# Sums of key-value features times query features: one 128-column product, or two 64-column products on the two halves of the array

## The chip, the cores and the metric

The kernel runs on one core of a Trainium2 chip. The metric is the device time of one execution in microseconds. The time before is 671.87 us, the median of three runs (671.34 to 672.88). One more execution was taken with the hardware profiler. It took 672.59 us, and every view of the profile below describes that execution.

## What is computed

A sequence of 2048 tokens with 512 features goes through a linear attention with 32 heads, and then through a mixture of eight experts of which each token uses one. All numbers are float32. The part that matters here, cut from the reference:

```python
phi_q = concatenate([softmax(pq), softmax(-pq)])      # 32 features per head and token
phi_k = concatenate([softmax(pk), softmax(-pk)])
kv  = einsum("bhsf,bhsd->bhfd", phi_k, v)             # 32 x 16 per head, summed over tokens
z   = einsum("bhsf->bhf", phi_k)
num = einsum("bhqf,bhfd->bhqd", phi_q, kv)
den = einsum("bhqf,bhf->bhq", phi_q, z)[..., None] + 1e-6
o   = num / den                                       # then o @ wo, a residual, and the experts
```

The change is in how `num` and `den` are made.

## The kernel before

The work is in stages, on 16 chunks of 128 tokens. In the first stage each chunk is projected to queries, keys and values, the feature maps are taken, and the sums `kv` and `z` grow in PSUM (the products of line 640). The query features are transposed, so that the features lie along the partitions and the tokens along the columns, and kept in SBUF as `phT[c]`: eight groups of 128 features (four heads of 32 features each) by 128 tokens (line 650).

When the sums are complete, they are copied to `kvbd` (line 814): for each of the eight groups a block-diagonal matrix of 128 features by 68 columns, four heads with 16 values and one denominator each.

Then comes the stage of the change, one step for each chunk `c` (the loop of line 940). It is a pipeline by hand: step `c` issues `s_num(c)`, `s_ot(c-1)` and `s_wo(c-2)`.

- `s_num(c)` (line 472) makes numerators and denominators. For two halves `i` of the heads it takes a PSUM bank `pn`, and TensorE makes four products into it (line 478). In each, the 128 features by 128 tokens of `phT` stand in the array, and the 68 columns of `kvbd` move through it. The result has 128 tokens as partitions and 68 columns. VectorE then takes the reciprocal of the denominators (`den`, line 482) and multiplies (`o`, line 483).
- `s_ot(c)` (line 487) transposes `o` on TensorE (`pto`, line 442). ScalarE rounds the result to its high part `xh` (line 78) and VectorE takes the rest `xl` (line 81).
- `s_wo(c)` (line 826) multiplies with the output weights in three products of high and low parts for each piece (`po`, lines 84 to 86, 24 instructions for a chunk). VectorE adds the residual (`hb`, line 838), and ScalarE and GpSimd make the statistics of the second norm.

Between them lie the small products of the token ranking (`pl`, lines 886 and 887; `acc`, line 908). From step 10 on, the weights of the first expert are loaded (`raw`, lines 253 and 981) and split into high and low parts by ScalarE, VectorE and GpSimd (lines 78 and 210). The experts follow and take the rest of the time; of them only the transposes of line 1132 play a part in the prediction, four of which have 32 tokens in place of 128.

Each engine takes its instructions in order. TensorE's loading of a standing operand (LDWEIGHTS, "PEld" in the profile) has rows of its own beside those of the products ("PE"). A product of plain float32 operands, such as `pn`, shows as two load rows and two product rows, so the 128 products of line 478 are 256 rows of each. A product of the rounded parts, such as `po`, shows as one of each. In the views, a form such as `128*32` ahead of the shape is the part of the array that an instruction uses, rows by columns.

Of the kernel before, what the change touches and what calls it, by code (L numbers as in the profile page):

```python
# [49 lines left out]
def kernel(  # L50
# [14 lines left out]
    V, A, G, T = nc.vector, nc.scalar, nc.gpsimd, nc.tensor  # L65
# [65 lines left out]
    def bank(name):  # L131
        return ps.tile([P, 512], F32, name=name, tag="b")
# [244 lines left out]
    with ExitStack() as actx:  # L377
# [23 lines left out]
        phT = [None] * NT  # L401
        for i in (3, 2, 1, 0):
# [3 lines left out]
            if i == 3:  # L406
                wohi = pool.tile([P, KD, 2, HC], F32R, name="wohi")
                wolo = pool.tile([P, KD, 2, HC], F32R, name="wolo")
                kvbd = pool.tile([P, NG, VC], F32, name="kvbd")
# [8 lines left out]
        st = [dict() for _ in range(NT)]  # L418

        def row(name, bufs, tag):  # L420
            return work.tile([P, D], F32, name=name, tag=tag, bufs=bufs)

        def load_x(c, queue=nc.sync):
            st[c]["xt"] = row("xt", 3, "xt")
            queue.dma_start(st[c]["xt"], x[c * P:(c + 1) * P, :])
# [46 lines left out]
        def s_num(c):  # L472
            load_x(c)
            o = row("o", 2, "pc").rearrange("p (h f) -> p h f", f=DH)
            for i in range(2):
                pn = bank("pn")
                for g in range(4):
                    st[c]["pn"] = T.matmul(pn[:, g * 68:(g + 1) * 68], phT[c][:, 4 * i + g, :],
                                           kvbd[:, 4 * i + g, :], start=True, stop=True)
                nv = pn[:, 0:272].rearrange("p (h f) -> p h f", f=DH + 1)  # L480
                den = work.tile([P, 16, 1], F32, name="den")
                V.reciprocal(den, nv[:, :, DH:DH + 1])
                V.tensor_tensor(o[:, 16 * i:16 * i + 16, :], nv[:, :, 0:DH],
                                den.to_broadcast([P, 16, DH]), op=OP.mult)
            st[c]["o"] = o.rearrange("p h f -> p (h f)")
# [5 lines left out]
        if True:  # L491
# [319 lines left out]
            with after(pin["f1"]):  # L811
                for i in range(2):
                    for h in range(4):
                        pin["kv"] = V.tensor_tensor(kvbd[32 * h:32 * h + 32, 4 * i:4 * i + 4, 17 * h:17 * h + 17],
                                                    kvps[i][32 * h:32 * h + 32, :, 17 * h:17 * h + 17],
                                                    epsz[32 * h:32 * h + 32], op=OP.add)
            s_num(0)
            s_num(1)
            s_ot(0)
            with after(pin["kv"]):  # L820
# [119 lines left out]
        for c in range(NT + 8):  # L940
            if c > 1:
                at(s_num, c)
                at(s_ot, c - 1)
# [447 lines left out]
```

## Time and profile before

| what | value |
|---|---|
| time, median of three runs | 671.87 us (671.34 to 672.88) |
| time of the profiled execution | 672.59 us |
| its span, first to last instruction | 670.9 us |
| TensorE granted clock, mean over the span | 0.994 |
| products of line 478 | first starts at 194.3 us, last at 270.3 us |
| ScalarE busy, share of the span | 54% |
| GpSimd busy, share of the span | 33% |

The profiled execution took 1.69 us more than its span, which lies before the first and after the last instruction. A row of a timeline names the start, the length, the engine, the line of the code, the operation, the tiles written and read, the shape and how many instructions were merged into it. A row's length includes the time that the result takes to arrive, so the rows of successive products overlap. The pace, which is the time from one start to the next, says what a product costs when they follow each other.

### The profile page before, as it was taken

How to read it: one execution, taken by the hardware profiler on the slowest of the kernel's cores; microseconds unless marked ns; L12 is line 12 of the kernel's file. 1: busy time of each engine (PE TensorE's matmuls, PEld its weight loads, DVE VectorE, ACT ScalarE, POOL GpSimd, SP SyncE). 2: the span in 40 equal slices, each digit the busy share in tenths (PEclk: the TensorE clock that was granted, in tenths of full speed). 3: DMA queues.
4: the chain of work that ended last, by engine and by line, in shares of the span. 5: the costliest groups of instructions: out<-in, count | busy, mean ns of one | idle time of the engine just before them, and what ended most of it. 6: DMA issues, size and time to landing. Idle time of an engine off the chain costs nothing. (4 is left out here: it accounts for less than half of the span.)

```text
span 670.9 us, 12045 instructions
## 1 busy us (share of the span) xinstructions
PE 657.4 (98%) x4151; PEld 584.9 (87%) x4151; DVE 474.9 (71%) x903; ACT 361.0 (54%) x589; POOL 221.4 (33%) x294
## 2 busy tenths in 40 slices
PE   9999999999999999999999999999999999999994
PEld 8899999999999999867888888888888999999883
DVE  7997898877877677885132799995495657675961
ACT  6554445544324436745112688884485556675750
POOL 4576566666525345741100111121102111310210
PEclk9999999999999999999999999999999999999997
DMA  9522120100001429717600589996286636664620
GB/s 327 178 80 80 64 79 17 33 16 1 1 1 32 128 88 354 282 64 254 248 3 32 196 346 349 351 387 256 62 339 246 221 128 227 224 229 145 224 88 21
DMA packets 25804, 107.33 MB, mean 160 GB/s; under 512 B 3358, under 2 KB 3358, under 8 KB 16768
## 3 DMA queue, kind: packets, MB, share of 16 engines
q1 hardware_dynamic: 22096, 95.49, 39.5%
q0 software_dynamic: 3488, 10.92, 4.7%
q8 instruction: 35, 0.57, 0.3%
q14 instruction: 41, 0.34, 0.2%
q10 hardware_dynamic: 144, 0.02, 0.0%
HBM read 98.00 MB, written 8.81 MB: 159 GB/s over the span
## 5 line engine op out<-in xcount | busy, mean ns | idle before, releaser
L210 DVE TENSOR_TENSOR wlo<-raw,whi 128x1024 fp32r<-128x1024 f32 (+1 forms) x143 | 165.9, 1188 | 27.6 <-ACT whi L78 25.2
L78 ACT ACTIVATE whi<-raw 128x1024 fp32r<-128x1024 f32 (+1 forms) x148 | 145.3, 1007 | 32.7 <-PE mh L86 23.1
L161 POOL DMA_INDIRECT out_dram<-xg,sidx x15 | 18.1, 1206 | 186.6 <-DVE xg L1137 103.5
L601 POOL TENSOR_TENSOR ph<-t,sm 128x1024 f32<-128x1024 f32 x32 | 62.0, 1938 | 37.7 <-DVE sm L599 37.4
L589 ACT ACTIVATE t<-t,rstd 128x1024 f32<-128x1024 f32 x32 | 36.7, 1145 | 42.7 <-DVE t L588 42.7
L195 ACT ACTIVATE hs<-mh 128x512 f32<-128x512 f32 (+1 forms) x52 | 28.0, 538 | 50.7 <-PE mh L86 49.9
L84 PE MATMUL my<-whi,hA 128*128 128x512 f32 x120 | 50.1, 417 | 0.0
L149 POOL DMA_INDIRECT xg<-hbuf,gidx x22 | 27.0, 1226 | 64.6 <-DMA out_dram<-xg,sidx 46.4
L86 PE MATMUL my<-whi,hA 128*128 128x512 f32 x120 | 47.3, 394 | 0.0
L85 PE MATMUL my<-wlo,hA 128*128 128x512 f32 x120 | 47.1, 393 | 0.0
L594 DVE TENSOR_REDUCE sm<-t 128x64 f32<-128x1024 f32 x32 | 38.9, 1215 | 8.0 <-ACT t L589 5.2
L81 DVE TENSOR_TENSOR hA<-mtr,hA 128x512 fp32r<-128x512 f32 (+1 forms) x38 | 22.7, 597 | 30.5 <-ACTq L1061 15.8
L84 PE MATMUL mh<-whi,xhi 128*128 128x512 f32 (+1 forms) x112 | 42.6, 381 | 0.0
L86 PE MATMUL mh<-whi,xlo 128*128 128x512 f32 (+1 forms) x112 | 41.2, 368 | 0.0
L85 PE MATMUL mh<-wlo,xhi 128*128 128x512 f32 (+1 forms) x112 | 41.2, 367 | 0.0
L84 PE MATMUL po<-wohi,xh 128*128 128x260 f32 x128 | 37.4, 293 | 0.7 <-ACT xh L78 0.6
L84 PE MATMUL pv<-wvhi,xh 128*128 128x260 f32 x128 | 36.4, 284 | 0.0
L85 PE MATMUL po<-wolo,xh 128*128 128x260 f32 x128 | 36.3, 284 | 0.0
L86 PE MATMUL po<-wohi,xl 128*128 128x260 f32 x128 | 36.3, 285 | 0.0
L85 PE MATMUL pv<-wvlo,xh 128*128 128x260 f32 x128 | 36.3, 283 | 0.0
L86 PE MATMUL pv<-wvhi,xl 128*128 128x260 f32 x128 | 36.2, 283 | 0.0
L84 PE MATMUL mh<-whi,xwh 128*128 128x512 f32 (+1 forms) x96 | 36.1, 376 | 0.0
(353 smaller groups left out, 1936.7 us busy)
## 6 DMA issues: line engine op xcount, KB each, us to landing
raw<-in_w_dram SPq DMA_DIRECT2D x70, 1024.0 KB, 5.5
xt<-in_x_dram SPq DMA_DIRECT2D x32, 256.0 KB, 2.8
hbuf<-hb SPq DMA_DIRECT2D x8, 515.0 KB, 3.5
xT<-in_xTs_dram SPq DMA_DIRECT2D x16, 256.0 KB, 2.7
phT<-in_wv_dram SPq DMA_DIRECT2D x4, 256.0 KB, 4.1
phT<-in_wqkT_dram SPq DMA_DIRECT2D x4, 256.0 KB, 5.1
phT<-in_wqkT_dram SPq DMA_DIRECT2D x2, 512.0 KB, 6.4
phT<-in_wo_dram SPq DMA_DIRECT2D x2, 512.0 KB, 8.1
```

Of the source, the lines that this page charges most:

```text
L78: return A.activation(dst, src, AF.Copy)
L81: return V.tensor_tensor(dst, src, hi.bitcast(F32), op=OP.subtract)
L84: T.matmul(ps, ahi, bhi, start=first, stop=False)
L85: T.matmul(ps, ahi, blo, start=False, stop=False)
L86: return T.matmul(ps, alo, bhi, start=False, stop=last)
L149: G.indirect_dma_start(out=dst[0:n, :], out_offset=None, in_=hbuf if col else hbuf[0:S // 2, :], in_offset=bass.IndirectOffsetOnAxis(ap=gi ...
L161: m = G.indirect_dma_start(out=out, out_offset=bass.IndirectOffsetOnAxis(ap=sidx[0:n, col:col + 1], axis=0), in_=src[0:n, 0:D], in_offset= ...
L195: return A.activation(hs[c % 2][:, 0:fw], p[:, 0:fw], AF.Silu)
L210: return eng.tensor_tensor(lo, r, h.bitcast(F32), op=OP.subtract)
L589: A.activation(t, t, AF.Exp, scale=st[c]["rstd"])
L594: m = V.tensor_reduce(sm, t, AX.X, OP.add)
L601: pin["f2"] = G.tensor_tensor(ph.rearrange("p (a f) -> p a f", f=DH), t, bc(sm, DH), op=OP.mult)
```

## The change

In `s_num` each product of 128 standing tokens becomes two of 64. The first has the tokens 0 to 63 standing and writes the partitions 0 to 63 of `pn`. The second has the tokens 64 to 127 and writes the partitions 64 to 127. The moving operand, 68 columns of `kvbd`, is the same for both. The results are the same numbers at the same places. Nothing else is touched.

```diff
             for i in range(2):
                 pn = bank("pn")
                 for g in range(4):
-                    st[c]["pn"] = T.matmul(pn[:, g * 68:(g + 1) * 68], phT[c][:, 4 * i + g, :],
-                                           kvbd[:, 4 * i + g, :], start=True, stop=True)
+                    for s in range(2):
+                        r = slice(64 * s, 64 * s + 64)
+                        st[c]["pn"] = T.matmul(pn[r, g * 68:(g + 1) * 68], phT[c][:, 4 * i + g, r],
+                                               kvbd[:, 4 * i + g, :], start=True, stop=True)
```

## The prediction

> **What bounds the kernel now.** I read the page first, then the stretch of the changed stage by windows, then TensorE's waits there, then single blocks of the timeline. The page's first rows:
>
> ```profile
> PE 657.4 (98%) x4151; PEld 584.9 (87%) x4151; DVE 474.9 (71%) x903; ACT 361.0 (54%) x589; POOL 221.4 (33%) x294
> ```
>
> TensorE is busy 98% of the span. That is an average, so the stage itself has to be asked. The windows below are successive steps of the chunk loop, each from the start of one chunk's `pn` products to the next. Columns: window, its length, busy time and rows of each engine, granted clock, DMA share, GB/s.
>
> ```profile
> core 0: us, PE busy (x) PEld busy (x) DVE busy (x) ACT busy (x) POOL busy (x), PEclk, DMA share, GB/s
> 221.02:226.29 5.27, 5.27 (x51) 5.22 (x49) 4.24 (x20) 2.02 (x5) 1.42 (x6) 1.00 0.21 50
> 226.29:231.53 5.24, 5.24 (x51) 5.20 (x49) 2.89 (x11) 2.02 (x5) 3.12 (x9) 1.00 0.39 119
> ...
> 263.29:268.58 5.29, 5.29 (x52) 5.23 (x50) 4.75 (x17) 5.29 (x13) 3.64 (x9) 1.00 1.01 349
> 268.58:273.81 5.23, 5.23 (x52) 5.19 (x49) 5.09 (x20) 3.51 (x9) 3.71 (x9) 1.00 1.00 416
> ```
>
> A step takes 5.2 to 5.3 us, PE is busy in all of it at full clock, and the next engine, DVE, in 55 to 97%. TensorE's waits from 180 to 300 us are one wait of 0.6 us and one of 0.3:
>
> ```profile
> PE po L84 <- ACT xh L78: 0.6, 1, 0.6
> PE selp L300 <- DVE raw L294: 0.3, 1, 0.3
> ```
>
> So in this stage TensorE sets the end, and time taken from or given to it there moves everything behind it. Next, what sets the pace of the changed products. One block (eight products, 16 rows), its loads, and what stands around it:
>
> ```profile
> 214.95 1.90 PE L478 MATMUL pn<-kvbd,phT 128*128 128x68 f32 x16
> 216.68 0.60 PE L442 MATMUL pto<-ident,o 128*128 128x128 f32 x4
> ```
>
> ```profile
> 214.83 1.87 PEld L478 LDWEIGHTS pn<-kvbd,phT 128*128 128x128 f32 x16
> ```
>
> Next pn's own rows in the view of the tile, with least, median and greatest length in ns, and a long run of plain float32 products:
>
> ```profile
> L478 PEld LDWEIGHTS pn<-kvbd,phT x256: 187/192/193, 194.1 to 270.2; 128*128 128x128 f32 x128
> L478 PE MATMUL pn<-kvbd,phT x256: 222/275/307, 194.3 to 270.3; 128*128 128x68 f32 x128
> ```
>
> ```profile
> 297.82 5.31 PE L1199 MATMUL my<-raw,raw 128*128 128x512 f32 x12
> ```
>
> The block's pace is (1.90 - 0.275) / 15 = 108 ns for a load and a pass. A pass over 512 moving columns goes at (5.31 - 0.593) / 11 = 429 ns, with the 593 ns of one such row, quoted here:
>
> ```profile
> L1199 PE MATMUL my<-raw,raw 128*128 128x512 f32 x16 | 7.2, 593 | 0.0
> ```
>
> That is 0.838 ns a column, so 68 columns stream in 57 ns. The streaming therefore fills only half of the 108 ns. The other candidate is the load of 128 standing columns, whose rows fill the block just as closely: (1.87 - 0.192) / 15 = 112 ns. **The products are bound by their loads**, and a moving operand of 68 columns is too short to cover them. That 275 ns is the median and 222 the least says the same: 53 ns of a usual row are waiting.
>
> **The change part by part.** It removes 256 loads of 128 columns and their 256 passes. It adds 512 loads of 64 columns and 512 passes over the same 68 columns. No wait, queue entry, DMA or work of another engine is added or moved; `den` still waits for the bank's last product.
>
> Removed: 256 x 108 ns = 27.7 us of TensorE's path, all of it uncovered.
>
> Added, the loads. No row has 64 standing columns. The nearest rows are the transposes of line 1132:
>
> ```profile
> L1132 PEld LDWEIGHTS yw<-ident,raw 128*128 128x128 f32 x16 | 1.9, 141 | 0.0
> ...
> L1132 PEld LDWEIGHTS yw<-ident,raw 128*32 128x32 f32 x8 | 0.8, 96 | 0.3
> ```
>
> A load of 32 columns is 45 ns shorter than one of 128, so a narrow load costs less, column by column. I take half of 108 ns: 54 ns for 64 columns, between 108 (no saving, which the rows speak against) and nothing (wholly under other work).
>
> Added, the passes: 57 ns each, by the column rate. Transposes of 128 columns go at (0.60 - 0.275) / 3 = 108 ns against 128 x 0.838 = 107, so a pass costs 1 or 2 ns beside its columns; I take 59. Handing over a load and a product is no bound, as four small products show, 27 ns apart:
>
> ```profile
> 220.91 0.18 PE L886 MATMUL pl<-oh,tri 128*128 128x8 bf16 x1
> ...
> 220.99 0.17 PE L887 MATMUL pl<-cum,ones 128*128 128x8 bf16 x1
> ```
>
> Everything now hangs on whether the two halves work at the same time. No row of this trace has two parts of the array in turn, so the price of 512 narrow pairs is bounded from both sides. If both loads and passes of one half run beside those of the other, two rows fit in 59 ns: 512 x 59 / 2 = 15.1 us, 12.6 us less than now. If the halves take turns, each row costs the longer of 54 and 59 ns: 512 x 59 = 30.2 us, 2.5 us more than now. The break-even is 27.7 / 512 = 54 ns a row. I take the first, since the two halves share neither a column of the array nor a partition of `pn`, and since TensorE already works on a load and a pass at once on the very same columns (1.87 and 1.90 us in one stretch above).
>
> The Trainium skill, TensorEngine Tiling (Array Packing), section Key Properties, says that different tiles of the array can load and multiply in parallel; by that rule the time is the first end. No run here shows it yet.
>
> Of those 12.6 us not all arrives. In the lead-in, the first transposes wait for VectorE's `o`:
>
> ```profile
> 193.07 1.92 DVE L814 TENSOR_TENSOR kvbd<-kvps,epsz 32x68 f32<-32x68 f32 x8 [1.77 <-PE kvps L640]
> 195.33 0.26 DVE L482 RECIPROCAL den<-pn 128x16 f32<-128x16 f32 x1 [0.34 <-PE pn L478]
> 195.51 0.63 DVE L583 TENSOR_REDUCE mn<-pq 128x32 f32<-128x512 f32 x1
> 196.17 0.43 DVE L483 TENSOR_TENSOR o<-pn,den 128x256 f32<-128x256 f32 x1
> ...
> 197.30 0.69 DVE L483 TENSOR_TENSOR o<-pn,den 128x256 f32<-128x256 f32 x2
> ```
>
> ```profile
> 197.81 0.62 PE L442 MATMUL pto<-ident,o 128*128 128x128 f32 x4
> ```
>
> The two first blocks would be 1.6 us shorter. VectorE is free of `kvbd` at 194.99, and two reciprocals (0.26 each), the minimum (0.63) and two products (0.43 each) take 2.0 us, so the transposes can start at 197.0 in place of 197.81: 0.8 of 1.6 us is lost. In the last two steps quoted above, ScalarE is busy for 5.29 of 5.29 us and VectorE for 5.09 of 5.23: of 2 x 0.79 us gained there I count 0.2 as kept and 1.4 as lost. In the steps like the first quoted one, VectorE's 4.24 us stand against a new step of 5.27 - 0.79 = 4.48 us. It fits, at 95%, but a transpose will now and then wait: I take 1.0 us for the seven such steps, between nothing and 5.5 (all of their gain). The first expert's weights are hidden as long as their landing leads their use. One wait for them stands already:
>
> ```profile
> ACT whi L78 <- DMA raw<-in_w_dram: 1.3, 1, 1.3
> ```
>
> It can grow by what steps 10 and 11 gain, 1.6 us, on ScalarE, which has 3 us idle in such a step; I add nothing.
>
> Sum: 12.6 - 0.8 - 1.4 - 1.0 = 9.4 us less. The profiled execution's 672.59 us, 670.9 of span and 1.69 around it, becomes 663.2. The median of the runs is 0.72 us below it, so the forecast in its terms is 671.87 - 9.4 = **662.5 us**.
>
> **The rivals.** About 0.2%, 1.3 us, is what a measurement of this kernel can tell from no change.
>
> *The halves take turns.* For it: nothing in the trace shows two passes at once; successive passes start no sooner than their columns need. Against it: those all used the same columns. Price as worked out, +2.5 us: 674.4. With the border cost below at its measured end, +4.3: 676.2. It decides from 54 ns a row on. This is the case on the other side.
>
> *Loads take turns, passes overlap.* The loads are one chain in every row so far, at 108 ns for 128 columns. Two of 64 in turn are the same 108, so the stage is unchanged: 0 to +0.8 us with 1 or 2 ns for each added load, 671.9 to 672.7. The change would then do nothing that can be measured, though it does what it says.
>
> *The array drains where its division changes.* There are 15 blocks (the first two adjoin), so 30 borders. The trace has such borders. Columns, entering and leaving `128*32`:
>
> ```profile
> 576.79 0.29 PE L86 MATMUL yt<-hA,wlo 128*128 128x288 f32 x1
> ...
> 576.92 0.60 PE L1132 MATMUL yw<-ident,raw 128*32 128x128 f32 x4
> ...
> 577.28 0.38 PE L84 MATMUL gw<-xwh,whi 128*128 128x288 f32 x1
> ```
>
> Entering takes 0.13 us, as between the `yt` before. The last transpose starts at 576.92 + 0.60 - 0.27 = 577.25, and 0.03 us later the next product does, so this border costs nothing. Rows, leaving `32*128`:
>
> ```profile
> 517.16 0.43 PE L1074 MATMUL mtr<-ident,xn 32*128 32x32 f32 x4
> ...
> 517.52 0.50 PE L84 MATMUL my<-whi,hThi 128*128 128x512 f32 x1
> ```
>
> Here the last starts at 517.16 + 0.43 - 0.22 = 517.37 and the next 0.15 us later, 0.12 more than above; for 15 exits 1.8 us. A full drain is the length of a short product, 0.17 us (the small products above): 30 x 0.17 = 5.1 us. On top of taking turns this gives 671.87 + 2.5 + 5.1 = 679.5; with the halves overlapped it would cut the gain to 4.3.
>
> The same list of Key Properties in the Trainium skill states that changing the tiling mode drains TensorE. The column border above disagrees at 0.03 us, the row border is between.
>
> *Each change of half drains.* Two passes and a drain for each of 256 half products, 2 x 57 + 168 = 282 ns against 108 now: 256 x 174 ns = +44.5 us, 716. No row speaks for it.
>
> *Loads are not hidden under passes.* Each row then costs 54 + 57 = 111 ns: 512 x 111 = 56.8, +29.1 us, 701. The `pn` block speaks against it, where loads and passes of the same rows overlap today.
>
> The Trainium skill, TensorE: Matmul & The Clock Gate, section Part 3, says that loads overlap running products only where the row groups differ, and the two halves share all rows; the block disagrees for whole-array loads.
>
> **How the numbers follow.** Overlapped halves 0.42; turns 0.26; loads in turn 0.16; borders drain 0.07; every change drains 0.07; loads unhidden 0.02. The likeliest one's own range is 659.3 (all 12.6 kept) to 667.6 (the full drain at borders). The wanted range reaches from there through the loads in turn to the turns with the row border's price: 659.3 to 676.2, which holds 0.84. Faster by over 0.2%: 0.42. Within: 0.16. Slower: 0.26 + 0.07 + 0.07 + 0.02 = 0.42.
>
> **What would show it.** Rows of the form `128*64`, 512 of each kind. With overlap a block of a chunk lasts about 1.0 us in place of 1.7, steps take 4.5 us, and rows of successive half products start together in pairs. With turns a block lasts 1.9 us. With drains, gaps of 0.1 to 0.2 us stand at its ends or at each change of half. If blocks shrink but steps don't, VectorE's or ScalarE's rows fill the steps, and my sum of losses is wrong. If the load rows don't shorten from 192 ns towards 140, the halving of loads is wrong.

## The result, and the profile after

The changed kernel takes 667.45 us, the median of five runs (666.26 to 668.30), against 672.22 us for the kernel before in the same comparison. The ratio is 0.9925, with a 95% interval of 0.9914 to 0.9936: faster by 0.75%, about 5 us. The forecast was 9.4 us. The profiled execution took 666.93 us, 5.66 less than the one of before, with a span of 665.2 us. Of these, 0.36 us lie ahead of the changed stage: its first product starts at 193.93 in place of 194.29 us, though nothing ahead of it was changed.

The page's first row, TensorE's waits from 180 to 300 us, and the steps of the chunk loop by windows, all of the changed kernel (columns as in the prediction):

```profile
PE 650.2 (98%) x4407; PEld 574.0 (86%) x4407; DVE 473.8 (71%) x903; ACT 361.1 (54%) x589; POOL 221.4 (33%) x294
```

```profile
PE po L84 <- ACT xh L78: 1.2, 2, 0.6
PE po L84 <- DVE lg L841: 1.0, 1, 1.0
PE acc L910 <- DVE bm L903: 0.4, 1, 0.4
...
PE pn L480 <- DVE o L485: 0.3, 1, 0.3
```

```profile
core 0: us, PE busy (x) PEld busy (x) DVE busy (x) ACT busy (x) POOL busy (x), PEclk, DMA share, GB/s
218.13:222.82 4.69, 4.69 (x65) 4.47 (x62) 4.25 (x20) 2.02 (x5) 1.78 (x6) 1.00 0.20 69
222.82:227.49 4.67, 4.67 (x66) 4.53 (x64) 2.80 (x11) 2.02 (x5) 3.06 (x9) 1.00 0.33 109
...
256.29:262.85 6.56, 5.10 (x65) 4.51 (x62) 5.77 (x19) 6.56 (x16) 4.86 (x10) 1.00 1.03 339
262.85:268.41 5.56, 4.98 (x68) 4.64 (x66) 5.10 (x20) 2.92 (x8) 4.04 (x9) 1.00 0.99 402
```

Two things are to be seen. The middle steps take 4.69 us in place of 5.26, with TensorE still busy in all of them: 0.57 us gained a step. And step 14 (the window from 256.29) takes 6.56 us in place of 5.29, with ScalarE busy in all of it and TensorE in 5.10: there the change loses 1.27 us, and TensorE has waits of 2.9 us in the stage where it had 0.6.

The block itself, first in the kernel before and then in the changed one, with the last small product ahead of it and the transposes behind it:

```profile
221.02 1.98 PE L478 MATMUL pn<-kvbd,phT 128*128 128x68 f32 x16
222.84 0.60 PE L442 MATMUL pto<-ident,o 128*128 128x128 f32 x4
```

```profile
218.04 0.17 PE L889 MATMUL pl<-cum,ones 128*128 128x8 bf16 x1
218.13 1.17 PE L480 MATMUL pn<-kvbd,phT 128*64 128x68 f32 x32
219.23 0.66 PE L442 MATMUL pto<-ident,o 128*128 128x128 f32 x4
```

```profile
L480 PEld LDWEIGHTS pn<-kvbd,phT x512: 132/137/137, 193.9 to 263.7; 128*64 128x64 f32 x171
L480 PE MATMUL pn<-kvbd,phT x512: 222/223/273, 193.9 to 263.8; 128*64 128x68 f32 x171
```

The block holds 32 rows in place of 16 and lasts 1.10 us up to the transposes, in place of 1.82. Its pace is (1.17 - 0.223) / 31 = 30.5 ns a row, half of what one pass needs. A load row is 137 ns in place of 192, so 64 columns fewer save 55 ns. The median product row is 223 ns, the least of before: nothing waits for loads any more.

That two halves really run at once shows in this pace: two rows start in 61 ns, and 68 columns alone need 57. It shows as well in how many rows are in flight at one instant. Windows of 10 ns inside a block, product rows of `pn` alone; before, then the changed kernel, at the start of its block and further in:

```profile
221.50:221.51 0.01, 0.01 (x3) 1.00 0.00 0
```

```profile
218.20:218.21 0.01, 0.01 (x2) 1.00 0.53 205
218.27:218.28 0.01, 0.01 (x4) 1.00 0.53 205
...
218.50:218.51 0.01, 0.01 (x8) 1.00 0.53 205
218.70:218.71 0.01, 0.01 (x8) 1.00 0.00 0
```

A row lasts 223 ns. One half at 59 ns a row would have 3.8 rows in flight; eight are two halves side by side. The ends of product rows are modelled in the profile, so this count adds little to the pace; the starts say more. The count grows by two, because rows start in pairs, 6 to 7 ns apart, with 59 ns from pair to pair. That is the sign which the prediction had named.

### The profile page after: what moved, and what is told of

The parts are those of the page before. It is cut to its first block, busy times and chain, and to the rows that moved or that the text cites. A ratio compares the mean times of both kernels' runs of the same rounds, so it can differ in the third digit from the quotient of the medians.

```text
span 665.2 us, 12555 instructions
## 1 busy us (share of the span) xinstructions
PE 650.2 (98%) x4407; PEld 574.0 (86%) x4407; DVE 473.8 (71%) x903; ACT 361.1 (54%) x589; POOL 221.4 (33%) x294
## 5 line engine op out<-in xcount | busy, mean ns | idle before, releaser
L78 ACT ACTIVATE whi<-raw 128x1024 fp32r<-128x1024 f32 (+1 forms) x148 | 145.2, 1006 | 35.3 <-PE mh L86 22.5
L81 DVE TENSOR_TENSOR hA<-mtr,hA 128x512 fp32r<-128x512 f32 (+1 forms) x38 | 22.6, 596 | 30.5 <-ACTq L1063 15.8
```

What stands on the lines that cost most here:

```text
L78: return A.activation(dst, src, AF.Copy)
L81: return V.tensor_tensor(dst, src, hi.bitcast(F32), op=OP.subtract)
```

## The experiments

All ratios are to the kernel before, timed on the same chip. The first four kernels ask where the gain comes from, the other eight where the rest of it went.

**The same half in a row (e1_grouped).** The loops over halves and groups change places:

```diff
-                for g in range(4):
-                    for s in range(2):
+                for s in range(2):
+                    for g in range(4):
```

> In each bank the four products of the first half stand in a row, then the four of the second half; everything else is as in the changed kernel. Theory (two halves work side by side only where they alternate): rows of one half follow at 57 to 59 ns, a block of 32 rows takes 32 x 58 = 1.86 us and two borders of 0.1 us, 0.2 us more than the 128-column block of before, so 16 blocks give about +3.5 us, 675 to 677 us. Rival (narrow loads are what helps, alternation isn't needed): rows stay at 30 ns and the time at 667 us.

Measured: 670.08 us, 0.9966 (0.9952 to 0.9981), slower than the changed kernel and faster than before. A block, and the rows in flight at six instants of the one that starts at 224.29:

```profile
229.36 1.57 PE L480 MATMUL pn<-kvbd,phT 128*64 128x68 f32 x32
```

```profile
224.56:224.57 0.01, 0.01 (x4) 1.00 0.00 0
224.76:224.77 0.01, 0.01 (x7) 1.00 0.00 0
...
225.60:225.61 0.01, 0.01 (x4) 1.00 0.00 0
```

The pace is (1.57 - 0.223) / 31 = 43.5 ns, between 30.5 and 59. At the block's start and end four rows are in flight, as for one half alone, and in between six or seven, so even here the halves overlap for part of the time. Both expectations missed: alternation matters, but it seems that TensorE also starts rows of the second half while several of the first are still to come. The run answers one more rival, that a product of 64 columns simply passes in half the time: the order of the halves would then not matter, and the rows at the block's start, where one half is alone, wouldn't stand 59 to 60 ns apart.

**One bank of two (e2_first_bank).** `for s in range(n)` with `n = 2 if i == 0 else 1`, so that the second bank keeps products of 128.

> Only the first bank of each chunk has 64-column products, the second has 128-column ones. Theory (a gain by the row, and a fixed cost of about 0.2 us at the two borders of a block where the array's division changes): pace saves 0.37 us a step, borders cost 0.18 us, a step is 0.2 us shorter than before, about 5.05 us. Rival (no fixed cost, the smaller gain is in the rows themselves): half of the 0.57 us that the changed kernel's steps gain, a step of 4.97 us. Times: 669.5 to 670 against 668.5 to 669.

Measured: 671.40 us, 0.9981 (0.9971 to 0.9990). The steps:

```profile
221.44:226.56 5.12, 5.12 (x58) 4.90 (x55) 4.15 (x20) 2.02 (x5) 1.74 (x6) 1.00 0.16 53
226.56:231.65 5.09, 5.09 (x59) 4.95 (x57) 2.90 (x11) 2.02 (x5) 3.01 (x9) 1.00 0.38 117
```

They take 5.1 us, 0.15 less than before, not the 0.285 that half of the gain would be. With a gain `a` for all rows and a fixed cost `b` for a stretch, a - b = 0.57 and a/2 - b = 0.15, so a = 0.84 and b = 0.27 us. The theory of a fixed cost holds, and its size is nearer to 0.27 than to 0.18. The time gained, 0.2%, is less than either expectation had.

**Four strips (e3_quarters).** `for s in range(4)` and `r = slice(32 * s, 32 * s + 32)`.

> Four products of 32 standing columns in place of two of 64, on four strips of the array. Theory (two passes of a product follow each other in their strip, and only neighbours in the order overlap, or a row can't be issued faster): rows stay at about 30 ns, a block has 64 of them, 1.95 us, 0.97 more than with halves; 16 blocks give +14 us or more, 681 us. Rival (strips run freely beside each other, four at a time): 15 ns a row, the block as long as with halves, 667 us.

Measured: 668.10 us, 0.9919 (0.9902 to 0.9935), as the changed kernel. A block, and the rows in flight:

```profile
228.83 1.15 PE L480 MATMUL pn<-kvbd,phT 128*32 128x68 f32 x64
```

```profile
224.70:224.71 0.01, 0.01 (x16) 1.00 0.00 0
```

The pace is (1.15 - 0.223) / 63 = 14.7 ns, and sixteen rows are in flight. The theory fell and the rival holds: the strips run freely, and neither the order nor the issue of rows was the limit. Four rows take 59 ns, two rows took 61: with halves already, the moving columns set the pace, and narrower strips have nothing left to gain.

**The same for the sums over tokens (e4_kv_halves).** The products of line 640 write `kvps[g // 4][64 * s:64 * s + 64, ...]` from 64 columns of `ph` each, for `s` of 0 and 1.

> The changed kernel, with the products of line 640 (the sums over tokens, also 68 moving columns under 128 standing ones, also at 108 ns a row) split into two halves of the array in the same way. Theory (loads bound such products wherever TensorE sets the pace): 0.57 us a chunk as in the changed stage, 16 chunks, 9 us less than the changed kernel, about 658.5 us. Rival (VectorE, busy 87% there, takes over at once): 665 to 667 us.

Measured: 667.23 us, 0.9918 (0.9901 to 0.9934), no different from the changed kernel. TensorE's waits on GpSimd in that first stage, where the changed kernel has none:

```profile
PE ptq L652 <- POOL ph L603: 2.3, 4, 0.7
PE pv L86 <- POOL xl L573: 1.5, 2, 0.7
...
PE kvps L643 <- POOL ph L603: 1.2, 2, 0.7
```

The rival is nearly right in its time, with another engine than it named: TensorE now waits for GpSimd, most of all for its products of the features. The first `pn` product starts at 193.2 in place of 193.9 us, with the first of these sums at 35.3 us in both, so of 9 us some 0.7 arrives.

**The split of the expert's weights one step later, with the change and without (e5_shift, e6_shift_before).**

```diff
-            if NT - 4 <= c < NT:
+            if NT - 3 <= c <= NT:
...
-                        hi_piece(c - NT + 4, i, 4)
+                        hi_piece(c - NT + 3, i, 4)
```

The low parts (`LOS`) move by one step as well.

> The changed kernel, with the splitting of the first expert's weights (the high parts on ScalarE, the low parts on VectorE and GpSimd) one step of the chunk loop later: steps 13 to 16 in place of 12 to 15. Theory (ScalarE's wait for these weights, 3.8 us in the changed kernel against 1.3 before, stands ahead of xh in its queue, and TensorE idles for it in steps 14 and 15): ScalarE's wait falls under 1 us, step 14 comes down from 6.56 us to about 5, and the time falls by 1 to 2 us to 665.5 to 666.5. Rival (ScalarE and VectorE are simply full in these steps, 6.56 and 5.77 us of 6.56): the work only moves on to step 16 and the time stays at 667.5, or rises.

> The same shift by one step in the kernel before, as a control. Theory: TensorE did not idle for this wait there, so nothing is gained: 672 to 673 us, within 0.2% of the kernel before. Rival (the shift helps by itself, whatever the change): 1 to 2 us less than the kernel before.

Why this was tried is seen in ScalarE's rows of the changed kernel, and in its wait there (1.3 us before):

```profile
249.18 0.58 ACT L78 ACTIVATE xh<-pto 128x512 fp32r<-128x512 f32 x1
253.54 1.15 ACT L78 ACTIVATE whi<-raw 128x512 fp32r<-128x512 f32 x2 [3.79 <-DMA raw<-in_w_dram]
...
256.96 0.57 ACT L78 ACTIVATE xh<-pto 128x512 fp32r<-128x512 f32 x1
```

The transposes that the last of these reads started at 252.72 us and were done at 253.4. Their `xh` starts 3.6 us later: ahead of it in the queue stand four pieces of weights that landed only at 253.5, and statistics that these held up.

Measured: with the change 669.38 us, 0.9948 (0.9932 to 0.9965), by the ratios some 1.5 us slower than the changed kernel, though the two intervals just touch. Without it 675.23 us, 1.0035 (1.0024 to 1.0047): the control isn't neutral, the shift costs by itself, against both expectations. The trace of the first, with the starts of steps 14 and 15, then VectorE, TensorE and the clock in step 15:

```profile
255.73 1.17 PE L480 MATMUL pn<-kvbd,phT 128*64 128x68 f32 x32
...
260.42 1.17 PE L480 MATMUL pn<-kvbd,phT 128*64 128x68 f32 x32
```

```profile
264.88 0.69 DVE L840 TENSOR_TENSOR hb<-po,xt 128x512 f32<-128x512 f32 x1 [2.89 <-DMA xt<-in_x_dram]
```

```profile
266.87 0.80 PE L84 MATMUL po<-wohi,xh 128*128 128x260 f32 x2 [3.24 <-DVE o L485]
```

```profile
263.00:266.00 3.00, 0.63 (x6) 0.42 (x4) 1.12 (x5) 0.39 (x1) 0.90 (x2) 0.92 0.91 299
266.00:269.00 3.00, 2.13 (x10) 2.13 (x11) 2.28 (x7) 3.00 (x8) 1.47 (x5) 0.50 0.98 410
269.00:272.00 3.00, 3.00 (x19) 2.90 (x18) 1.91 (x13) 2.24 (x6) 1.36 (x3) 0.50 1.11 410
```

ScalarE's wait for the weights is gone, and step 14 takes 4.69 us in place of 6.56. The `xh` of step 13 stands ahead of the first pieces there. So it is pieces that wait ahead of this `xh` in ScalarE's queue that cost step 14: this half of the theory is shown. But step 15 pays it back. VectorE waits 2.89 us for a transfer of `x` behind the weights, TensorE idles 3.24 us, and its granted clock is 0.50 for the next 6 us. The wait was removed and another took its place.

**Fewer stretches (e7_pairs, e8_pairs_shift).**

```diff
-                at(s_num, c)
-                at(s_ot, c - 1)
+                at(load_x, c)
+                at(s_ot, c - 1)
+                if c % 2 == 0:
+                    at(s_num, c)
+                    at(s_num, c + 1)
```

> The changed kernel, with the numerators of two chunks made in one stretch at every second step, after the transposes, so that the array's division changes half as often: some 8 stretches in place of 15. The loads of x stay one step each. Theory (a fixed cost of about 0.18 us for each stretch of 64-column products): 7 x 0.18 = 1.3 us less in the steps, two successive steps take 9.2 us in place of 9.36, and the time is 666 to 667 us. Rival (the border costs nothing, and the steps' gain of 0.57 us in place of 0.75 has another reason): two steps stay at 9.36 us or grow by waits for PSUM banks, and the time is 667.5 or more.

> The changed kernel with both: numerators of two chunks in one stretch, and the splitting one step later. Theory (the two losses are separate): both gains add up, 2.5 to 3.5 us less than the changed kernel, 664 to 665 us. Rival (the later steps are bound by ScalarE and VectorE): no more than the better of the two alone.

Measured: 673.07 us, 1.0007 (0.9995 to 1.0020), and with the shift 672.32 us, 0.9997 (0.9986 to 1.0008). All of the gain is gone. Two pairs of steps of the first:

```profile
219.54:228.96 9.42, 9.42 (x128) 9.03 (x127) 6.49 (x31) 4.15 (x11) 4.80 (x14) 1.00 0.38 113
228.96:238.49 9.53, 9.53 (x130) 9.07 (x127) 7.13 (x31) 3.49 (x9) 3.68 (x12) 1.00 0.27 84
```

Two steps take 9.4 to 9.5 us, no less than 9.36, though the border is there half as often. Later steps were worse: ScalarE's wait for the weights is 4.9 us. The new order changed more than the number of borders, so this pair doesn't settle their cost; e2_first_bank does. The rivals were right in the times; together the two edits are slower than the shift alone.

**Fewer transfers in the loop (e9_loads, e10_loads_shift, e11_loads_before).** The transfers of line 981 move from steps 13 and 15 to 16 and 17: with the change, with the change and the shift, and in the kernel before.

> The changed kernel, with the last three of the first expert's seven weight transfers (1 MB each, used only behind the chunk loop) issued at steps 16 and 17 in place of 13 and 15. Theory (from step 12 on the DMA, full at 1.0 of its share, sets the pace of the chunk loop: first weights and x land late, and that takes the gain of the last steps back): from the issue of the first weights to the first product of the expert 27 us in place of 29, the time 665 to 666 us. Rival (ScalarE and VectorE are full there, the DMA only looks full): 29 us as before the shift, 667.5 us.

> Both: the three transfers later, and the splitting one step later as in the run with the shift alone. Theory (that run lost by the late landing of x, 2.9 us of VectorE's wait and then a slower TensorE clock): the wait for x goes, step 15 takes about 5 us in place of 9.6, the time is 664.5 to 666.5 us. Rival (engines are full, whatever the DMA does): 668 to 670 us as with the shift alone.

> The three transfers later in the kernel before, as a control. Theory: TensorE was the bound of the chunk loop there, so nothing moves: 672 to 673 us. Rival (later transfers help or hurt by themselves): more than 0.2% from the kernel before.

Measured: 667.29 us, 0.9918 (0.9904 to 0.9932); 667.29 us, 0.9923 (0.9909 to 0.9936); 671.85 us, 0.9992 (0.9983 to 1.0001). The control is neutral. Alone the edit gains nothing that can be told apart from the changed kernel: ScalarE's wait for the first weights is still 3.9 us, since it is for the first transfer, not for the last three. With the shift it takes 1.7 us, by the ratios, off that kernel's time, which is between the two expectations, and VectorE's wait for `x` falls from 2.9 to 1.4 us. So the full DMA is part of what the shift ran into, but not the whole, and the theory that it sets the pace of the last steps by itself fell.

**No splits in the loop (e12_no_splits_in_loop).** The pieces were to follow the last `po`, after the loop's own splits were left out.

> The changed kernel, with all splitting of the first expert's weights that lay in steps 12 to 15 moved behind the loop. The total must grow, since the expert then waits for the splits; only steps 12 to 15 are read. Theory (ScalarE's wait for the weights and the splits in its and VectorE's queues are what TensorE idles for): steps 13 to 15 take 4.7 us like those before. Rival (the late landing of x through the full DMA is enough by itself): some of these steps stay over 5.2 us.

Measured: 667.48 us, one run. The edit did not do what it was for. ScalarE still has the pieces in its queue inside the loop, and the same wait:

```profile
253.83 1.15 ACT L78 ACTIVATE whi<-raw 128x512 fp32r<-128x512 f32 x2 [3.76 <-DMA raw<-in_w_dram]
```

Step 14 takes 8.7 us, from 256.60 to 265.28. The run tells nothing about the loop without splits, which so wasn't tried.

## Why the prediction was right, and where it was off

**The likeliest case happened.** The prediction put 0.42 on two halves that run side by side, and that is what the rows in flight and the pace of 30.5 ns show. It is also the rule of the Trainium skill, TensorEngine Tiling (Array Packing), section Key Properties, that tiles load and multiply in parallel; the eight rows in flight agree. The diagnosis that loads of 128 columns bound these products was right too: the narrow loads are 55 ns shorter, and product rows no longer wait. The rivals with halves or loads in turn are out, and so are a drain at each change of half and loads that aren't hidden. The measured 5 us is a little over half of the 9.4 forecast. 667.45 us lies just inside the likeliest case's own range, 659.3 to 667.6, at the end that it gave to a full drain at each border. The terms of the sum say why.

**The rows.** Forecast 12.6 us, from 27.7 removed and 15.1 added. Measured: 512 x 30.5 ns are 15.6 us, and all blocks before, each from its first product to the next other product, are 28.6 us together. The prediction had taken its 108 ns from a block of 1.73 us; those of the middle steps take 1.79 to 1.82. So 13.0 us, and this term is nearly right.

**The border.** The prediction took nothing, from the border of the transposes of 32 columns, and named 1.8 to 5.1 us as what it would cost otherwise. Measured: in a middle step the rows of a block save 1.82 - 32 x 0.0305 = 0.84 us, and the step 0.57. That leaves 0.27 for a stretch, as e2_first_bank has it. The rows show where most of it lies. The first narrow product starts 0.09 us behind the last small one (0.03 before). The first transpose starts 0.15 us behind the last narrow row, where a pair needs 0.06, and the four transposes last 0.66 us in place of 0.60. The load for the first transpose, before and then changed:

```profile
222.73 0.47 PEld L442 LDWEIGHTS pto<-ident,o 128*128 128x128 f32 x4
```

```profile
219.23 0.31 PEld L442 LDWEIGHTS pto<-ident,o 128*128 128x128 f32 x3
```

Before, it started 0.11 us ahead of the transpose, under the last products; in the changed kernel it starts with it. At 0.21 us, as these rows add up, to 0.27, 15 stretches cost 3.2 to 4.1 us. This is the step that failed most: the rival "the array drains where its division changes" was half true, beside the likeliest case and not in place of it. What misled was the border of the transposes: the form `128*32` says how many columns an instruction uses, and whether the array was divided for them no row shows. The Trainium skill, TensorEngine Tiling (Array Packing), section Key Properties, says that a change of the tiling mode drains TensorE. The measurement agrees in kind: 0.10 to 0.14 us a border, near the 0.12 of the row border in the prediction.

**VectorE in the middle steps.** Forecast a loss of 1.0 us. There was none: the steps take 4.69 us each with TensorE busy throughout, although VectorE is busy for 4.25 of them.

**The last steps.** Forecast 1.4 us lost, and for the first weights the prediction said "I add nothing", because ScalarE had 3 us idle in such a step. That was wrong in kind. ScalarE takes its queue in order, so idle time behind a waiting instruction hides nothing. The wait grew from 1.3 to 3.8 us, and the shift shows that what it held up ahead of `xh` made step 14 long. The size of the whole loss is read from three rows of each kernel, before and then changed: the start of step 12, the issue of the first weights and the expert's first product.

```profile
252.63 1.98 PE L478 MATMUL pn<-kvbd,phT 128*128 128x68 f32 x16
```

```profile
252.78 2.07 SPq L253 DMA_DIRECT2D raw<-in_w_dram  x4
```

```profile
281.81 0.48 PE L84 MATMUL mh<-whi,xhi 128*128 128x512 f32 x1
```

```profile
246.33 1.17 PE L480 MATMUL pn<-kvbd,phT 128*64 128x68 f32 x32
```

```profile
247.32 2.15 SPq L253 DMA_DIRECT2D raw<-in_w_dram  x4
```

```profile
276.27 0.48 PE L84 MATMUL mh<-whi,xhi 128*128 128x512 f32 x1
```

The changed kernel is 6.3 us ahead at the start of step 12, 5.5 when it issues the loads and 5.5 when the expert begins; from the issue on both need 29.0 us. So from step 12 on it loses 0.8 us, where four steps at 0.57 would have given 2.3: 3.0 us lost in place of 1.4.

Part of this has a cause that the prediction ruled out ("No wait, queue entry, DMA or work of another engine is added or moved"). ScalarE's instructions stand in another order. Before, `xh` stands ahead of the second pass of the norm's statistics (`junk`, line 849); in the changed kernel it stands behind it, and that pass waits for GpSimd. Step 11, before, then the changed kernel on ScalarE and on VectorE:

```profile
249.71 0.60 ACT L78 ACTIVATE xh<-pto 128x512 fp32r<-128x512 f32 x1 [0.91 <-PE pto L442]
250.20 0.71 ACT L849 ACTIVATE junk<-hb,hnm 128x512 f32<-128x512 f32 x1
```

```profile
243.96 0.72 ACT L851 ACTIVATE junk<-hb,hnm 128x512 f32<-128x512 f32 x1 [0.99 <-POOL hnm L850]
...
244.69 0.58 ACT L78 ACTIVATE xh<-pto 128x512 fp32r<-128x512 f32 x1
```

```profile
245.29 0.69 DVE L81 TENSOR_TENSOR xl<-pto,xh 128x512 fp32r<-128x512 f32 x1 [1.05 <-ACT xh L78]
```

In the middle steps this costs nothing, since TensorE is busy throughout. In step 11 the choice of the first expert stands behind `xl` in VectorE's queue, and the loads wait for the choice: they are issued 4.68 us behind the start of the step's transposes (242.64 us) in place of 3.71 (249.07). These lines of the code are the same in both kernels, so the order seems to have come about when the program was built. No run here holds it fixed, so its share of the loss isn't known.

**The sum, as measured.** The lead-in lost about 1.0 us, 0.8 forecast: from the first `pn` product to the third block it takes 8.29 us in place of 9.30, 1.0 less, where the rows give 2.5 and the borders of two stretches take 0.5. So 13.0 us of rows, less 1.0 for the lead-in, 3.2 to 4.1 for borders and 3.0 for the last steps, leaves 4.9 to 5.8. From the first `pn` product to the expert's first product the changed kernel takes 82.34 us in place of 87.52, which is 5.2 less.

**What stays open.** What else than ScalarE's wait holds the last steps isn't settled, the new order in ScalarE's queue included. Moving the splits or the transfers, or both, gave 29.5 to 31.1 us in place of 29.0 for that stretch, never less. No kernel tried here is clearly faster than the changed one.

## What to carry to other kernels

When a load of standing columns is longer than the pass that should cover it, try the standing operand split over two parts of the array in turn: here the passes then set the pace, and finer strips added nothing. Count the borders where the array's division changes, some 0.2 to 0.3 us for a stretch here, and make the stretch long enough. And when the bounding engine gets faster, look for the next in-order queue with a transfer wait in it: its idle time is not slack for what stands behind the wait. Compare the order of the other engines' instructions too, for a change on one engine can move it.

## What the runs showed of the hardware

- With 32 columns in each of four strips, product rows followed at 14.7 ns and sixteen were in flight, in e3_quarters; the 27 ns of the small products in the prediction isn't a floor of issue.
- In the changed kernel a border of a 64-column stretch cost 0.10 to 0.14 us; the load for the first product behind it began only with that product.
- In e1_grouped, seven rows were in flight where the code has eight rows of one half and then eight of the other. The Trainium skill, TensorE: Matmul & The Clock Gate, section Part 3, says that products start and end strictly in order. With strict order and 59 ns from row to row in a half, only the last row of one half could start beside the first of the next, and at most five rows would be in flight. This run doesn't seem to fit that; which half a row belongs to, the trace doesn't say.
- After TensorE had idled for 3.24 us in e5_shift, its granted clock was 0.50 for two windows of 3 us.
